# Scale products on GpSimd, two buffers for a split, and one attention step taken apart, in an attention and feed-forward kernel

## The chip, the cores and the metric

The kernel runs on one core of a Trainium2 chip. The metric is device microseconds of one execution: 1246.51 as the median of three runs (1242.34 to 1246.77). One further execution was profiled, and every line of a profile here comes from such an execution.

[...]

## The reference

```python
# q, k, v: (8, 12, 448, 64) float32; w_in (768, 2048), w_out (2048, 768)
scores = scale * np.matmul(q, k.transpose(0, 1, 3, 2)) - np.log(S)   # scale = 1/8, S = 448
attn = 1.0 / (1.0 + np.exp(-scores))
x = np.matmul(attn, v)          # then heads side by side: (3584, 768)
h = x @ w_in
g = h - np.tanh(h)
return g @ w_out
```

Attention with a sigmoid in place of a softmax, in 8 batches of 12 heads, and then a feed-forward layer on the 3584 tokens.

## The kernel before

**Exact products from halves.** A float32 operand is scaled by a power of two and split into two float16 halves, high and low; a product is made as three float16 matmuls (high by high, high by low, low by high) that add up in PSUM. Each operand so needs a scale. For a pair of heads, `norms` (L302) squares q, k and v on ACT with running sums and `scales` (L311) makes the powers of two: PE adds over partitions (`pbn`, L316), ACT applies a Relu (L318), and DVE makes `n_y`, `in`, `sn` and `rn` in five tiny instructions of one to three columns. `parts` (L332) splits K or Q into the tile `w` (one buffer) and has a DMA transpose it; `prep_v` (L348) splits v.

**Stages.** Batch 0's attention is done first, in float32 (`attention32`), while the weights are loaded and converted. Then come, for each batch, the first product (`moe1`, x by w_in, followed by the nonlinearity `mix` on ACT and DVE) and the second (`moe2`, g by w_out). The attention of the next batch is woven into the second product. `stream` (L434) is a generator that yields it in blocks. There are six head pairs in a batch and two blocks to a pair. A block has the scores of two of a pair's four column groups on PE, two sigmoids on ACT (`weigh`) and, from batch 2 on, their splits into `ahl` on ACT and DVE (L382, L383); batch 1's products with v are made in float32. The products of v with finished weights (`do_av`) come in every block for batch 1, and from batch 2 on in a pair's first block (i = 0), for the pair before; after a pair's fourth column group ACT evacuates x and squares it, and POOL adds the squares up (L431). So the last products with v of a batch are in the first block of the next batch's scores.

**The order.** It is written by hand: each of PE, ACT, DVE and POOL runs its instructions in program order. `second` (L937) steps through the second product, one yield for 6 products, and calls the blocks, the tail of `mix` and the preparation of the next x at given steps (`BLOCKS0` in batch 0, `BLOCKS1` in batch 1, `BLOCKS` later). A token tile of 128 tokens ends at steps 16, 32 and 48 in batches 1 to 7: there ACT empties one PSUM tile `po` (L825) and DVE the other (L826); PE has only these two buffers, and goes on into the same two. The last 64 tokens (`por`, L834) fill the rest, at two yields to a step. Three steps after the block that ends a batch's attention, `batch_scales` (L606) makes that batch's scale and splits its six x tiles into `xhl`, the first product's operand. The bound for g, `g_scales` (L631), is worked out after the first `mix`.

**Weights.** w_out is converted during batch 0: `conv_load`, `conv_sign`, `conv_bits`, and a PE product `wl` (L178) for its norm; `w_out_scale` makes its scale and `split` its halves in place, `SHIFT_O` slots ahead of the raw form.

What the diff touches, with the line numbers of the profile:

Of the kernel before, what the change touches and what calls it, by code (L numbers as in the profile page):

```python
# [34 lines left out]
class Builder:  # L35
# [58 lines left out]
    def pow2(self, t, n, tag):  # L94

        nc = self.nc
        y = self.sm.tile([P, n], F32, name=f"{tag}_y", tag=f"{tag}_y")
        nc.vector.tensor_scalar(
            y.bitcast(U32), t.bitcast(U32), 24, 23, op0=ALU.logical_shift_right, op1=ALU.logical_shift_left
        )  # L100
        return y


# [55 lines left out]
    def conv_norm(self, p):  # L159
        nc = self.nc  # L160
        k = p["k"]
        if not p["staged"]:
            return
        p["sq"] = self.sm.tile([P, p["piece"][3]], BF16, name="sq", tag="sq", bufs=4)
# [60 lines left out]
    def scale_of(self, total, tag):  # L225

        nc = self.nc
        t = self.sm.tile([P, 1], F32, name=tag + "_t")
        nc.vector.tensor_scalar(t, total, 2.1, TINY, op0=ALU.mult, op1=ALU.max)
        y = self.pow2(t, 1, tag)  # L230
        inv = self.const.tile([P, 1], F32, name=tag + "_i")
        nc.vector.tensor_scalar(inv, y, 2.0**49, None, op0=ALU.mult)
        S = self.const.tile([P, 1], F32, name=tag + "_s")
        nc.vector.reciprocal(S, inv)
        return S, inv
# [23 lines left out]
    def w_out_scale(self, e):  # L259

        V = self.nc.vector
        m = self.sm.tile([P, 1], F32, name="mo")
        V.tensor_reduce(m, self.wl[:, : self.HALF], axis=AX.X, op=ALU.max)
        total = self.sm.tile([P, 1], F32, name="wtot2")
        V.scalar_tensor_tensor(total, m, 1.05, m, op0=ALU.mult, op1=ALU.mult)
# [36 lines left out]
    def norms(self, loaded):  # L302

        n = len(loaded)
        ss = self.sm.tile([CK, 3], F32, name="ss", bufs=3)
        for i, t in enumerate(loaded):
            junk = self.sm.tile([CK, 8 * D], BF16, name="sqn", tag="sq", bufs=4)
            self.nc.scalar.activation(junk, t.rearrange("p a b d -> p (a b d)"), AF.Square, accum_out=ss[:, i : i + 1])  # L308
        return ss[:, :n]

    def scales(self, ss):  # L311

        nc = self.nc
        n = ss.shape[1]
        pb = self.ps.tile([P, 512], F32, name="pbn", tag="tr", bufs=1)[:, :n]
        nc.tensor.matmul(pb, self.onesf[:CK, :], ss, start=True, stop=True)  # L316
        t = self.sm.tile([P, 3], F32, name="tn")
        nc.scalar.activation(t[:, :n], pb, AF.Relu, bias=self.tiny, scale=2.1)  # L318
        y = self.pow2(t[:, :n], n, "n")
        i = self.sm.tile([P, 3], F32, name="in")  # L320
        nc.vector.tensor_scalar(i[:, :n], y, 2.0**49, None, op0=ALU.mult)
        s = self.sm.tile([P, 3], F32, name="sn", bufs=3)
        nc.vector.reciprocal(s[:, :n], i[:, :n])
        r = self.sm.tile([P, 2], F32, name="rn", bufs=5)
        nc.vector.scalar_tensor_tensor(
            r[:, 0:1], i[:, 0:1], 1.0 / math.sqrt(D), i[:, 1:2], op0=ALU.mult, op1=ALU.mult
        )
        if n == 3:
            nc.vector.tensor_scalar(r[:, 1:2], y[:, 2:3], 2.0**49 / A_SCALE, None, op0=ALU.mult)
        return s, r  # L330

    def parts(self, n, s, name, act):  # L332

        nc = self.nc
        flat = n.rearrange("p c h d -> p (c h d)")
        w = self.qk.tile([CK, 2, 4 * P], F16, name="w", tag="w", bufs=1)
        if act:
            nc.scalar.activation(w[:, 0], flat, AF.Copy, scale=s[:CK])  # L338
# [95 lines left out]
    def stream(self):  # L434
# [171 lines left out]
    def batch_scales(self, xs):  # L606
# [3 lines left out]
        t1 = lambda name: self.sm.tile([P, 1], F32, name=name)  # L610
        tx = t1("tx")
        V.tensor_scalar(tx, m, 2.12, TINY, op0=ALU.mult, op1=ALU.max)
        y = self.pow2(tx, 1, "x")
        ix = t1("ix")
        V.tensor_scalar(ix, y, 2.0**49, None, op0=ALU.mult)
        Sx = t1("Sx")
        V.reciprocal(Sx, ix)
        xhl = []
        for j, x in enumerate(xs):
# [5 lines left out]
            xhl.append(hl)  # L625
        ih, ihk = t1("ih"), t1("ihk")
        V.tensor_tensor(ih, ix, self.iSwi, op=ALU.mult)
        V.tensor_scalar(ihk, ih, KAPPA, None, op0=ALU.mult)
        self.xready = (xhl, ih, ihk, m)

    def g_scales(self, m):  # L631

        t1 = lambda name: self.sm.tile([P, 1], F32, name=name)
        V = self.nc.vector
# [7 lines left out]
        V.scalar_tensor_tensor(h3, h2, 1.0 / 9.0, hc, op0=ALU.mult, op1=ALU.mult)  # L642
        g2 = t1("g2")
        V.tensor_tensor(g2, hb, h3, op=ALU.min)
        V.tensor_scalar(g2, g2, 2.1, TINY, op0=ALU.mult, op1=ALU.max)
        y = self.pow2(g2, 1, "g")
        iSg = t1("iSg")
        V.tensor_scalar(iSg, y, 2.0**49, None, op0=ALU.mult)
        Sg = t1("Sg")
        V.reciprocal(Sg, iSg)  # L650
        return Sg, iSg
# [9 lines left out]
    def moe1(self, st):  # L661

        nc = self.nc
        S = self.S
        xhl, ih, ihk, m = st
        self.gs = []
        self.late = []
        for k in range(self.NF // 2):
# [18 lines left out]
            for _ in self.tail:  # L687
                pass
            if k == 0:
                self.Sg, self.iSg = self.g_scales(m)  # L690

    def moe1_32(self, xs, weights, rest):
# [6 lines left out]
        for k in range(self.NF // 2):  # L699
            ph = self.ps.tile([P, 2, 512], F32, name="ph", tag="sc", bufs=2)  # L700
            for e in range(2):
# [17 lines left out]
                elif (k, e) == (1, 0):  # L719
                    next(w, None)  # L720
                    self.Sg, self.iSg = self.g_scales(m)
                if e == 0 and k in self.INIT:
# [47 lines left out]
    def moe2(self, b, gs):  # L770
# [3 lines left out]
        n = 1 if b == 0 else 3  # L774
        nc.vector.tensor_scalar(iK[:, :n], self.iSwo[:, :n], self.iSg, None, op0=ALU.mult)
        H = self.HALF
# [27 lines left out]
        if b == 0:  # L804
            for e in range(2):
                for tk in range(nt):
                    po = {e: self.ps.tile([P, 512], F32, name="po", tag="mm", bufs=2)}
                    for f in range(0, self.NF, 2):
                        products(po, tk, f, (e,))
                        products(po, tk, f + 1, (e,))  # L810
                        if f + 2 == self.NF:
                            if (e, tk) == (1, 0):
                                nc.vector.tensor_scalar(iK[:, 1:], self.iSwo[:, 1:], self.iSg, None, op0=ALU.mult)
                            o = self.op.tile([P, H], F32, name="oh", tag="o", bufs=2)
# [67 lines left out]
    def first(self, rest):  # L882

        n = 4
        next(self.tail)
        ahead = [self.split_w_out(0)]
        for k in range(n):
# [11 lines left out]
        next(rest)  # L899
        assert n + len(self.BLOCKS0) + len(self.BLOCKS1) == 4 * self.NP + len(self.BLOCKS) - self.ALONE  # L900
        split = self.split_w_in()
# [35 lines left out]
    def second(self, b, blocks, alone, events):  # L937
# [49 lines left out]
```

## Time and profile before

| | us |
|---|---|
| median of three runs | 1246.51 (1242.34 to 1246.77) |
| profiled execution, whole | 1250.16 |
| its span, first to last instruction | 1247.9 |
| PE busy in the span | 1202.3 |
| DVE busy | 941.6 |
| ACT busy | 942.0 |
| POOL busy | 38.0 |

The span is what the rows of the profile cover; 2.26 us of the execution lie around it. Batch 0 with the weights takes until 276 us, where batch 1's first product starts; later batches take some 142 us each. A row of a timeline has the start, the duration (of several alike together, with their count), the engine, the line of the kernel, the operation, output and inputs, and in brackets how long the engine had stood idle and which instruction ended the wait. A row of waits has the waiting engine and line, the instruction that released it, and the sum, the count and the longest in us. A row of a window has the window, its length, the busy time of PE, PE's weight loads, DVE, ACT and POOL, then the granted TensorE clock (1.00 is full speed), the transfers' share and GB/s.

### The profile page before, as it was taken

The page shows a single profiled execution, that of the slowest core. Times are in us where ns is not written, and L with a number is a line of the kernel's source. Part 1 is how long each engine was busy: PE and PEld are TensorE (multiplying, and loading weights), DVE is VectorE, ACT ScalarE, POOL GpSimd, SP SyncE. Part 2 cuts the span into 40 slices and gives each one's busy share as a digit, 9 for nine tenths or more (in the row PEclk, how much of TensorE's full clock was granted, in tenths as well). Part 3 has the DMA queues.
Part 4 walks back from the last instruction along what each step waited for, and adds up shares of the span by engine and source line. Part 5 has one row for each costly group of instructions (what it writes and reads, how often), then busy time and mean ns, then how long its engine had stood idle before and what let it go on. Part 6 is the DMA issues. An engine that isn't in the chain of part 4 may idle for free.

```text
span 1247.9 us, 19830 instructions
## 1 busy us (share of the span) xinstructions
PE 1202.3 (96%) x7675; PEld 651.9 (52%) x7675; DVE 941.6 (75%) x1473; ACT 942.0 (75%) x1325; POOL 38.0 (3%) x38
## 2 busy tenths in 40 slices
PE   9889887999999999999999999999999999999998
PEld 3235433455555555555555555555555655555555
DVE  4879987888966798668976789668985789636930
ACT  5857796967998688886888788886888877864820
POOL 0100000000000000100001000000000000000000
PEclk9999989999999999999999999999999999999999
DMA  9963358220044400432034400552024410300001
GB/s 241 282 171 83 89 124 208 64 61 8 4 111 100 92 1 13 107 93 57 1 65 108 95 2 1 102 110 57 1 55 100 89 25 1 72 21 20 1 14 32
DMA packets 192317, 89.76 MB, mean 72 GB/s; under 512 B 169824, under 2 KB 182368, under 8 KB 192224
## 3 DMA queue, kind: packets, MB, share of 16 engines
q1 hardware_dynamic: 191296, 88.28, 30.4%
q8 instruction: 60, 0.98, 0.3%
q10 hardware_dynamic: 928, 0.23, 0.1%
q14 instruction: 33, 0.27, 0.1%
HBM read 58.20 MB, written 11.01 MB: 55 GB/s over the span
## 4 chain that ended last, share of the span: by engine, by line
PE 71%; DVE 11%; ACT 10%; DMA 4%; issue 3%; SPq 1%; DVEq 0%; ACTq 0%
PE ph L674 31%; PE po L796 22%; PE sc L367 6%; PE acc L391 5%; PE por L834 5%; DMA raw<-moe_w_in 2%; ACT a L376 2%; ACT ahl L382 1%; ACT sqn L308 1%; DVE ahl L383 1%; DVE m L748 1%; DVE m L762 1%; DVE m L759 1%; DVE g L659 1%; DMA K<-w 1%
## 5 line engine op out<-in xcount | busy, mean ns | idle before, releaser
L796 PE MATMUL po<-wo,g 128*128 128x384 f16 x2304 | 394.1, 327 | 7.5 <-DVE o L826 4.9
L674 PE MATMUL ph<-xhl,wi 128*128 128x448 f16 x2016 | 382.6, 352 | 0.0
L796 PEld LDWEIGHTS <-g 128*128 128x128 f16 x2304 | 220.1, 98 | 183.5 <-issue 43.4
L674 PEld LDWEIGHTS <-wi 128*128 128x128 f16 x2016 | 196.7, 98 | 185.0 <-issue 1.8
L383 DVE SCALAR_TENSOR_TENSOR ahl<-a,ahl 112x896 f16<-112x896 f32 x144 | 155.7, 1122 | 68.6 <-ACT ahl L382 68.5
L376 ACT ACTIVATE a<-sc,nls,rn 112x896 f32<-112x896 f32 x168 | 179.5, 1092 | 18.7 <-PE sc L367 18.2
L744 ACT ACTIVATE u<-ph,ih 128x896 f32<-128x896 f32 x64 | 64.4, 1006 | 91.6 <-PE ph L674 87.9
L382 ACT ACTIVATE ahl<-a 112x896 f16<-112x896 f32 x144 | 128.3, 941 | 0.1
L367 PE MATMUL sc<-Q,K 64*112 64x448 f16 x1008 | 116.2, 361 | 8.9 <-ACT a L376 7.3
L748 DVE SCALAR_TENSOR_TENSOR m<-ph,ihk,u 128x896 f32<-128x896 f32 x64 | 73.4, 1147 | 38.0 <-ACT th L746 37.7
L658 ACT ACTIVATE g<-m,Sg 128x896 f16<-128x896 f32 x64 | 66.7, 1042 | 32.7 <-DVE m L762 27.3
L391 PE MATMUL acc<-ahl,vhl 112*64 112x448 f16 x864 | 89.0, 355 | 0.8 <-DVE ahl L383 0.8
L367 PEld LDWEIGHTS <-K 64*112 64x112 f16 x1008 | 60.9, 128 | 47.5 <-issue 27.8
L341 DVE SCALAR_TENSOR_TENSOR w<-qn,sn,w 112x512 f16<-112x512 f32 x42 | 31.5, 750 | 70.5 <-ACT w L338 70.2
L762 DVE COPY_PREDICATED m<-u,th 128x896 f32<-128x896 uint32 x64 | 77.3, 1208 | 6.6
L659 DVE SCALAR_TENSOR_TENSOR g<-m,Sg,g 128x896 f16<-128x896 f32 x64 | 73.3, 1146 | 8.5 <-ACT g L658 8.4
L704 PE MATMUL ph<-x,wi 128*128 128x448 f32 x192 | 76.5, 549 | 0.0
L759 DVE SCALAR_TENSOR_TENSOR m<-q,m 128x896 f32<-128x896 f32 x64 | 70.0, 1093 | 8.3 <-ACT q L758 1.2
L749 DVE SCALAR_TENSOR_TENSOR th<-ph,ih,th 128x896 f32<-128x896 f32 x64 | 73.2, 1143 | 0.0
L761 ACT ACTIVATE u<-u,b 128x896 f32<-128x896 f32 x64 | 66.8, 1044 | 6.4 <-DVE m L748 4.4
L755 DVE SCALAR_TENSOR_TENSOR m<-q,m 128x896 f32<-128x896 f32 x64 | 69.5, 1086 | 0.0
L391 PEld LDWEIGHTS <-vhl 112*64 112x64 f16 x864 | 46.0, 110 | 40.6 <-issue 13.4
(130 smaller groups left out, 1236.3 us busy)
## 6 DMA issues: line engine op xcount, KB each, us to landing
raw<-moe_w_in SPq DMA_DIRECT2D x24, 512.0 KB, 8.3
rawo<-moe_w_out SPq DMA_DIRECT2D x32, 384.0 KB, 4.1
kn<-k SPq DMA_DIRECT2D x96, 112.0 KB, 2.8
vn<-v SPq DMA_DIRECT2D x48, 224.0 KB, 3.1
qn<-q SPq DMA_DIRECT2D x94, 112.0 KB, 2.9
out<-o SPq DMA_DIRECT2D x7, 336.0 KB, 2.7
out<-o SPq DMA_DIRECT2D x7, 288.0 KB, 2.7
out<-o SPq DMA_DIRECT2D x7, 240.0 KB, 3.2
```

The costliest lines, as they stand in the source:

```text
L367: nc.tensor.matmul(ps[:CK, h, :S], K[r, w, cs], Q[r, x, :], start=(n == 0), stop=(n == len(prods) - 1))
L376: nc.scalar.activation(a, ps[:CK, :, :S], AF.Sigmoid, bias=self.nls[:CK], scale=scale)
L382: nc.scalar.activation(A[:, 0], a, AF.Copy, scale=A_SCALE)
L383: nc.vector.scalar_tensor_tensor(A[:, 1], a, A_SCALE, A[:, 0], op0=ALU.mult, op1=ALU.subtract)
L391: nc.tensor.matmul(acc[h * D : (h + 1) * D, : self.S], v[:, w, h, c, :], A[:, x, h], start=(c == 0 and n == 0), stop=(c == 3 and n == 2),)
L659: nc.vector.scalar_tensor_tensor(g[:, 1], m, Sg, g[:, 0], op0=ALU.mult, op1=ALU.subtract)
L674: nc.tensor.matmul(ph[:, e, :S], self.wi[:, c * self.NB + k, part, e * P : (e + 1) * P], xhl[c][:, x, :], start=(i == 0), stop=(i == 3 * s ...
L704: nc.tensor.matmul(ph[:, e, :S], self.where("in", c)[:, f * P : (f + 1) * P], xs[c], start=(c == 0), stop=(c == self.NC - 1),)
L748: V.scalar_tensor_tensor(m, ps, ihk, u, op0=ALU.mult, op1=ALU.mult)
L759: V.scalar_tensor_tensor(m, q2, C2, m, op0=ALU.add, op1=ALU.mult)
L762: V.copy_predicated(m, u.bitcast(U32), th)
L796: nc.tensor.matmul(po[i][:, :H], gs[f // 2][:, x, f % 2, tk * P : (tk + 1) * P], self.wo[:, i * self.NF + f, w], start=(f == 0 and n == 0) ...
```

## The change

- The constants of the scale chains are made from the power of two `y` by one bitwise xor on DVE and products on GpSimd (`over`, and `V = nc.gpsimd` in `scales`, `scale_of`, `w_out_scale`, `batch_scales`, `g_bound`, `g_scales`, `moe2`), in place of a reciprocal and products on DVE.
- `scales` for the pair after next is called in a pair's first block, behind `do_av` and ahead of `prep_v`, in place of at the start of its second block.
- `g_scales` is cut in two, `g_bound` (GpSimd) and `g_scales`, and both are called in `batch_scales` ahead of the splits of x. The splits then follow 1, 3 and 5 steps after the norms in place of 0, 2 and 4.
- `w` shares two buffers of another pool with the squares of the weight conversion; the discarded squares of `norms` go to PSUM; `SHIFT_O` is 4.
- `w_out_scale(0)` is called after the first part of the last `mix` in place of ahead of it.
- Batch 1's last products with v are a step of their own, without scores, and the block with batch 2's first scores comes as the first block of batch 1's second product: `BLOCKS1` has one more entry.

```diff
-    BLOCKS1 = (4, 7, 10, 13, 16, 20, 24, 28, 32, 36, 40, 44, 48, 52)
+    BLOCKS1 = (4, 7, 10, 13, 16, 19, 22, 25, 28, 32, 36, 40, 44, 48, 52)
-    SHIFT_O = 3
+    SHIFT_O = 4
...
+    def over(self, out, y):
+
+        z = self.sm.tile([P, 3], F32, name="z")[:, : y.shape[1]]
+        self.nc.vector.tensor_scalar(z.bitcast(U32), y.bitcast(U32), 0x7F800000, None, op0=ALU.bitwise_xor)
+        self.nc.gpsimd.tensor_scalar(out, z, 2.0**-50, None, op0=ALU.mult)
...
+        junk = self.ps.tile([P, 512], F32, name="sqn", tag="tr", bufs=1)
         for i, t in enumerate(loaded):
-            junk = self.sm.tile([CK, 8 * D], BF16, name="sqn", tag="sq", bufs=4)
...
+        V = nc.gpsimd
         y = self.pow2(t[:, :n], n, "n")
+        s = self.sm.tile([P, 3], F32, name="sn", bufs=3)
+        self.over(s[:, :n], y)
         i = self.sm.tile([P, 3], F32, name="in")
-        nc.vector.tensor_scalar(i[:, :n], y, 2.0**49, None, op0=ALU.mult)
-        s = self.sm.tile([P, 3], F32, name="sn", bufs=3)
-        nc.vector.reciprocal(s[:, :n], i[:, :n])
+        V.tensor_scalar(i[:, :n], y, 2.0**49, None, op0=ALU.mult)
...
-        w = self.qk.tile([CK, 2, 4 * P], F16, name="w", tag="w", bufs=1)
+        w = self.sm.tile([CK, 2, 4 * P], F16, name="w", tag="sq", bufs=2)
...
             for i in range(2):
-                if i:
-                    scales(g + 2)
                 pss = [self.scores(c, K[g], Q[g]) for c in (2 * i, 2 * i + 1)]
...
                 if i == 0 or not splits(g):
                     do_av()
                 if i == 0:
+                    scales(g + 2)
                     if g == 0:
                         prep_v(0)
                     prep_v(g + 1)
...
                 yield 2750, True
+                if i and g == NP - 1:
+                    do_av()
+                    yield 1900, False
...
+        ih, ihk = t1("ih"), t1("ihk")
+        G.tensor_tensor(ih, ix, self.iSwi, op=ALU.mult)
+        G.tensor_scalar(ihk, ih, KAPPA, None, op0=ALU.mult)
+        g = self.g_bound(m)
+        yield 0
+        sg = self.g_scales(g)
         xhl = []
...
-            if k == 0:
-                self.Sg, self.iSg = self.g_scales(m)
...
-                    self.w_out_scale(0)
...
         next(self.tail)
+        self.w_out_scale(0)
...
-            events += [(p, lambda: next(scales[0], None)) for p in (end + 5, end + 7)]
+            events += [(p, lambda: next(scales[0], None)) for p in (end + 4, end + 6, end + 8)]
```

More of the change, by code (lines that the diff above doesn't have):

```diff
@@ L94, in pow2 @@
     def pow2(self, t, n, tag):
-        nc = self.nc
         y = self.sm.tile([P, n], F32, name=f"{tag}_y", tag=f"{tag}_y")
-        nc.vector.tensor_scalar(
+        self.nc.vector.tensor_scalar(
             y.bitcast(U32), t.bitcast(U32), 24, 23, op0=ALU.logical_shift_right, op1=ALU.logical_shift_left
@@ L163, in conv_norm @@
             return
-        p["sq"] = self.sm.tile([P, p["piece"][3]], BF16, name="sq", tag="sq", bufs=4)
+        if k % 2 == 0:
+            self.sq2 = self.sm.tile([P, 2, p["piece"][3]], BF16, name="sq", tag="sq", bufs=2)
+        p["sq"] = self.sq2[:, k % 2]
         if k % 6 == 1:
@@ L611, in batch_scales @@
         tx = t1("tx")
+        G = self.nc.gpsimd
         V.tensor_scalar(tx, m, 2.12, TINY, op0=ALU.mult, op1=ALU.max)
         y = self.pow2(tx, 1, "x")
+        Sx = t1("Sx")
+        self.over(Sx, y)
         ix = t1("ix")
-        V.tensor_scalar(ix, y, 2.0**49, None, op0=ALU.mult)
-        Sx = t1("Sx")
-        V.reciprocal(Sx, ix)
+        G.tensor_scalar(ix, y, 2.0**49, None, op0=ALU.mult)
+        ih, ihk = t1("ih"), t1("ihk")
[4 more added lines that the diff above has]
+        sg = self.g_scales(g)
         xhl = []
@@ L625, in batch_scales, with g_bound @@
             xhl.append(hl)
[L626 to L631, printed above, removed]
+        self.xready = (xhl, ih, ihk, sg)
+    def g_bound(self, m):
         t1 = lambda name: self.sm.tile([P, 1], F32, name=name)
-        V = self.nc.vector
+        V = self.nc.gpsimd
         hb = t1("hb")
@@ L641, in g_scales @@
         h3 = t1("h3")
-        V.scalar_tensor_tensor(h3, h2, 1.0 / 9.0, hc, op0=ALU.mult, op1=ALU.mult)
+        V.tensor_scalar(h3, h2, hc, 1.0 / 9.0, op0=ALU.mult, op1=ALU.mult)
         g2 = t1("g2")
-        V.tensor_tensor(g2, hb, h3, op=ALU.min)
+        V.tensor_scalar(g2, hb, h3, None, op0=ALU.min)
         V.tensor_scalar(g2, g2, 2.1, TINY, op0=ALU.mult, op1=ALU.max)
+        return g2
+    def g_scales(self, g2):
+        t1 = lambda name: self.sm.tile([P, 1], F32, name=name)
+        V = self.nc.gpsimd
         y = self.pow2(g2, 1, "g")
+        Sg = t1("Sg")
+        self.over(Sg, y)
         iSg = t1("iSg")
         V.tensor_scalar(iSg, y, 2.0**49, None, op0=ALU.mult)
-        Sg = t1("Sg")
-        V.reciprocal(Sg, iSg)
         return Sg, iSg
@@ L664, in moe1 @@
         S = self.S
-        xhl, ih, ihk, m = st
+        xhl, ih, ihk, (self.Sg, self.iSg) = st
         self.gs = []
@@ L720, in moe1_32 @@
                     next(w, None)
-                    self.Sg, self.iSg = self.g_scales(m)
+                    g2 = self.g_bound(m)
+                elif (k, e) == (1, 1):
+                    self.Sg, self.iSg = self.g_scales(g2)
                 if e == 0 and k in self.INIT:
@@ L774, in moe2 @@
         n = 1 if b == 0 else 3
-        nc.vector.tensor_scalar(iK[:, :n], self.iSwo[:, :n], self.iSg, None, op0=ALU.mult)
+        nc.gpsimd.tensor_scalar(iK[:, :n], self.iSwo[:, :n], self.iSg, None, op0=ALU.mult)
         H = self.HALF
@@ L899, in first @@
         next(rest)
[L900 removed]
+        assert n + len(self.BLOCKS0) + len(self.BLOCKS1) == 4 * self.NP + len(self.BLOCKS) - self.ALONE + 1
         split = self.split_w_in()
```

24 lines of the change are left out of this document (11 added, 13 removed).

## The prediction

> **What bounds the kernel now.** I read the page first, then TensorE's waits, then the order of time around each wait. TensorE (PE) is the bound: it is busy 96% of the span, so a change pays only where PE stands idle or at a low clock, and costs wherever it makes PE stand.
>
> ```profile
> PE 1202.3 (96%) x7675; PEld 651.9 (52%) x7675; DVE 941.6 (75%) x1473; ACT 942.0 (75%) x1325; POOL 38.0 (3%) x38
> ```
>
> ```profile
> PE wl L178 <- DVE stb L152: 8.4, 8, 2.1
> PE sc L367 <- ACT a L376: 7.3, 5, 2.5
> PE sc L578 <- ACT a L376: 5.0, 6, 1.0
> PE po L796 <- DVE o L826: 4.9, 6, 1.3
> ```
>
> These are PE's largest waits. The third is batch 0's own attention, which the change leaves alone. The first two lie in batch 0's later part, while weights are converted. Rows of PE there, after one of ACT:
>
> ```profile
> 194.15 0.72 ACT L338 ACTIVATE w<-kn,sn 112x512 f16<-112x512 f32 x1 [3.65 <-DVE sn L323]
> ```
>
> ```profile
> 162.65 2.49 PE L367 MATMUL sc<-Q,K 64*112 64x448 f16 x12 [1.45 <-DVE th L749]
> ...
> 195.90 0.77 PE L367 MATMUL sc<-Q,K 64*112 64x448 f16 x6 [1.78 <-ACT a L376]
> ...
> 211.00 0.33 PE L178 MATMUL wl<-stb,onesb 128*128 128x384 bf16 x1 [1.35 <-DVE stb L152]
> ...
> 214.49 0.33 PE L178 MATMUL wl<-stb,onesb 128*128 128x384 bf16 x1 [2.18 <-DMA rawo<-moe_w_out]
> 214.75 2.27 PE L367 MATMUL sc<-Q,K 64*112 64x448 f16 x12
> ...
> 253.81 1.34 PE L367 MATMUL sc<-Q,K 64*112 64x448 f16 x12
> ...
> 260.97 0.35 PE L601 MATMUL nm<-x,onesb 128*128 128x448 bf16 x1 [0.94 <-ACT x L422]
> ```
>
> The 12 score matmuls of a block take 1.34 us at full clock (253.81). At 214.75 they take 2.27: after two waits near each other the clock is granted at half:
>
> ```profile
> 216.00:217.00 1.00, 1.00 (x8) 0.27 (x4) 0.88 (x2) 1.00 (x4) 0.00 (x0) 0.50 0.80 116
> ```
>
> The fourth wait above is the end of a token tile in the second product: PE wants the next pair of PSUM tiles, and ACT and DVE have still to empty them. Batch 1 pays most:
>
> ```profile
> 360.56 0.32 PE L796 MATMUL po<-wo,g 128*128 128x384 f16 x1 [1.25 <-ACT o L825]
> ...
> 362.17 5.37 PE L796 MATMUL po<-wo,g 128*128 128x384 f16 x23 [1.28 <-DVE o L826]
> ```
>
> Batch 2 at the same place, one query for each engine:
>
> ```profile
> 500.26 0.48 DVE L353 TENSOR_SCALAR vhl<-vn,sn 112x512 f16<-112x512 f32 x1
> 500.77 0.75 DVE L354 SCALAR_TENSOR_TENSOR vhl<-vn,sn,vhl 112x512 f16<-112x512 f32 x1
> 502.55 2.34 DVE L383 SCALAR_TENSOR_TENSOR ahl<-a,ahl 112x896 f16<-112x896 f32 x2 [1.02 <-ACT ahl L382]
> 504.81 0.60 DVE L826 TENSOR_SCALAR o<-po,iK 128x384 f32<-128x384 f32 x1
> ```
>
> ```profile
> 501.10 0.58 ACT L422 ACTIVATE x<-x 128x448 f32<-128x448 f32 x1
> 501.58 1.78 ACT L382 ACTIVATE ahl<-a 112x896 f16<-112x896 f32 x2
> ```
>
> ```profile
> 505.47 3.90 PE L796 MATMUL po<-wo,g 128*128 128x384 f16 x23 [0.59 <-DVE o L826]
> ```
>
> Here 23 products take 3.90 us; after batch 1's two waits 23 took 5.37, so a half clock costs 1.47 us more. DVE splits v (L353, L354) while ACT is still evacuating x, then idles 1.02 us until ACT's split of a, and only after its own two splits comes the o that PE waits for.
>
> **The change, part by part.** The sum is made against the profiled execution (1250.16 us, span 1247.9, 2.26 around it); that is 3.65 above the median of 1246.51, and I add the difference to the median.
>
> *Scale chains.* Each removes from DVE the products in, sn, rn and adds one xor:
>
> ```profile
> L323 DVE RECIPROCAL sn<-in 128x3 f32<-128x3 f32 (+1 forms) x42 | 7.3, 174 | 1.4
> L321 DVE TENSOR_SCALAR in<-n_y 128x3 f32<-128x3 f32 (+1 forms) x42 | 7.1, 170 | 1.4
> L98 DVE TENSOR_SCALAR n_y<-tn 128x3 uint32<-128x3 uint32 (+1 forms) x42 | 6.7, 160 | 0.0
> ```
>
> The reciprocal and product (0.174 + 0.170) minus a xor like L98's (0.16) give 0.18 us, times 42: 8 us of DVE, somewhat more with the rn rows. No PE wait in the products of batches 2 to 7 is in front of such a chain, so this is hidden under PE's work; I count 0. The same holds for g_scales, which leaves DVE in the first product, where PE waits for nothing.
>
> *Scales half a pair earlier.* In batch 0's later part it pays: ACT stood 3.65 us for sn at 194.15, and PE's 1.78 at 195.90 follows from it. With sn there a block before, that wait goes; ACT runs ahead, so the raw weight at 211.00 (1.35) should come in time. But DVE, which converts one weight piece a step, limits here too, and now stands for the chain behind ACT's evacuation. I take 1.5 of these 3.1.
>
> *w_out_scale(0) behind the last mix:* its chain no longer delays th, 1.45 at 162.65; ACT binds next, so I take 0.9. *Batch 1's last products with v alone:* the squares no longer queue behind the block's two sigmoids and a w, so 0.94 at 260.97 goes: 0.9. The 1.34 of scores moves to batch 1 and costs the same there: 0. With that block go its Q transpose and the loads of the pair three ahead, on SP's queue: they leave batch 0, where SP also feeds raw weights, and are wanted two blocks later in batch 1: 0. A half clock at 214.75 costs at least 2.27 - 1.34 = 0.93; if the waits before it shrink, it goes: 0.9, and about 0.8 of the 2.18. Together **batch 0: -5**, bounds 0 (DVE limits everything) and -9 (1.45 + 1.78 + 1.35 + 2.18 + 0.94 + 0.93 and the rest of the half clock).
>
> *Batch 1's tile end at step 16.* 1.25 + 1.28 + 1.47 = 4.0 us now. The block ahead of it changes from one with evacuation to one with three squares of norms, so ACT's o is no earlier; PE's own work ahead is a products-with-v shorter. Steps of 3 up to 28 keep ACT behind for twice as long. I take **-2**, bounds -4 and +1.
>
> *The order on DVE in batches 1 to 6, which costs.* In a block with evacuation DVE now has the scale chain in front of its split of v, and that chain waits for an ACT Relu put behind the evacuation and its square. So L353 and L354 (1.2 us), which lay in DVE's idle gap, start after 501.68 + Relu + chain (about 0.6): they end near 503.5, and the splits of a, which started at 502.55, start 1.0 later without any collision; 0.55 at least if ACT is a little earlier. And Pool's sum of squares collides:
>
> ```profile
> 202.66 1.14 POOL L431 TENSOR_TENSOR x<-x,x 128x448 f32<-128x448 f32 x1 [14.88 <-ACT x L422]
> ```
>
> ```profile
> 201.21 0.35 DVE L151 TENSOR_SCALAR stb<-stb 128x384 uint32<-128x384 uint32 x1
> ...
> 203.07 0.95 DVE L151 TENSOR_SCALAR stb<-stb 128x384 uint32<-128x384 uint32 x1 [0.32 <-PE po L796]
> ```
>
> A DVE tensor_scalar of 0.35 us took 0.95 beside Pool's sum. L353 would now stand beside that sum: up to 0.6 more, and tiny Pool products, which queue on Pool behind that sum (none in the trace; bounded by 0 and the 1.14 of a whole sum, taken near 0.1 as they have one to three columns) may add some. **Step 16, batches 2 to 6: +1.1 each, 5.5**, bounds 0.55 and 1.9. At step 32 there is some margin:
>
> ```profile
> 388.71 0.60 DVE L826 TENSOR_SCALAR o<-po,iK 128x384 f32<-128x384 f32 x1
> ```
>
> ```profile
> 389.60 4.08 PE L796 MATMUL po<-wo,g 128*128 128x384 f16 x24
> ```
>
> DVE's o ends at 389.31, PE needs the second tile just after 389.60: margin 0.4. **+0.7 each for five batches, 3.5**, bounds 0.1 and 1.5.
>
> *The end of batches 1 to 5.* The splits of x come in three parts at 48, 50, 52 in place of 47, 49, 51, and the last behind the whole block of 52:
>
> ```profile
> 568.12 0.68 DVE L624 SCALAR_TENSOR_TENSOR xhl<-x,Sx,xhl 128x448 f16<-128x448 f32 x1
> ```
>
> ```profile
> 569.53 10.77 PE L674 MATMUL ph<-xhl,wi 128*128 128x448 f16 x56
> ```
>
> The last split ends at 568.80. PE wants the sixth x after 15 matmuls of 10.77 / 56 = 0.19: 572.4. Ahead of the last two x now lie that block's w (0.75, as L354), v (0.48 + 0.75), a (2.3, the L383 row) and chain (0.3), and the block before has the 1.0 delay; the products moved off DVE give back about 1. So the last split ends near 568.8 + 4.6 + 1.0 - 1.0 = 573.4 and its second half is wanted at 572.6; ten dependent Pool products must also be through before DVE's bound for g, which stands ahead of the first x. **+1.5 each, 7.5**, bounds 0.5 and 2.5.
>
> *Two buffers for w, PSUM for the squares' waste, the shift of 4:* ACT's wait for K's transpose goes, under PE's work: 0; uncovered it would give ACT a microsecond a batch.
>
> Sum: -5 - 2 + 5.5 + 3.5 + 7.5 = +9.5, so 1256.
>
> **Rivals.** (1) *Slower, as above*: 1256, own range 1248 to 1267. (2) *Faster*: the stall of ACT for sn and the clock cuts that follow carry the day. Gains at their bounds, -9 and -4, against order costs at their floor, 5 x 0.55 + 5 x 0.1 + 5 x 0.5 = 6: -7, 1239.5. [...] It decides if DVE's o and last x move by less than half a microsecond. Against it: program order puts the split of v behind Relu. (3) *Even*: gains -7, costs at about 7: 1246.5. (4) *Much slower*: the step-16 wait of 0.59 + 1.1 = 1.7 cools the clock as in batch 1, 1.47 more in each of five batches: 1256 + 7 = 1263. Two waits of 1.25 and 1.28 within 2.9 us did it there; one of 1.78 at 195.90 did not.
>
> [...]
>
> **How the numbers follow.** Chances: 0.5 for 1256, 0.17 faster, 0.2 even, 0.13 much slower. What a measurement can tell from no change is 0.5%, 6.2 us: 1240.3 to 1252.7. A seventh of the first case lies under 1252.7 (0.07), rival 3 between, a little of rival 2 above 1240.3: faster 0.16, same 0.28, slower 0.56. The range for 8 in 10 reaches from 1239, inside the faster case, to 1266, past the middle of rival 4.
>
> **What would show it.** Right: PE's wait for DVE's o at step 16 grows from 0.59 to 1.5 or more, one appears at step 32, PE's first L674 of batches 2 to 6 waits for xhl, and L353 stands behind the chain's xor. Also: no ACT wait for sn near 190, no 0.94 at the norms of batch 1. Wrong: those o waits unchanged, the first product starting without a wait, or the half clock gone from batches 0 and 1 altogether.

## The result, and the profile after

The changed kernel takes 1265.86 us (median of four, 1265.32 to 1267.09), the kernel before 1244.97 beside it (1242.34 to 1246.77): a ratio of 1.0178, with a 95% interval of 1.0159 to 1.0197. The forecast had the direction, but +9.5 us where +20.9 came.

In the rows PE is TensorE, DVE VectorE, ACT ScalarE, POOL GpSimd and SP SyncE. The page's busy times and TensorE's waits in the changed kernel (waiting line, releaser, sum, count, longest in us). L813 is the second product (L796 before), L843 DVE's eviction `o` (L826), L373 the scores, L611 the reduction `m` of the norms, L639 the second half of a split of x:

```profile
PE 1210.2 (96%) x7675; PEld 646.2 (51%) x7675; DVE 934.2 (74%) x1260; ACT 946.4 (75%) x1325; POOL 198.5 (16%) x311
```

```profile
PE po L813 <- DVE o L843: 15.8, 10, 2.5
PE wl L185 <- DVE stb L157: 13.6, 10, 4.0
PE sc L373 <- ACT a L382: 4.2, 3, 2.9
PE ph L692 <- DVE xhl L639: 3.4, 10, 0.4
PE sc L373 <- DVE m L611: 2.0, 5, 0.4
```

DVE is less busy (934.2 against 941.6 us) and PE waits longer for it: 15.8 us in ten evictions against 4.9 in six. Two waits are new, for x and for `m`. POOL went from 38.0 to 198.5 us.

Batch by batch, from the start of one first product to that of the next (us, read from PE's timelines). "Before" is a second profile of the unchanged kernel (the run e11 below), because batch 0 took 276.0 in the first one:

| | batch 0 | 1 | 2 | 3 | 4 | 5 | 6 | 7 | span |
|---|---|---|---|---|---|---|---|---|---|
| before | 271.1 | 151.8 | 141.8 | 141.8 | 142.5 | 141.8 | 135.8 | 115.9 | 1242.6 |
| after | 267.0 | 155.9 | 146.8 | 146.8 | 146.8 | 146.8 | 138.5 | 115.9 | 1264.5 |
| difference | -4.1 | +4.1 | +5.0 | +5.0 | +4.3 | +5.0 | +2.7 | 0.0 | +21.9 |

What holds PE at step 16 of batch 2, in four timelines of the changed kernel; the same place as the prediction's rows from 500 to 505 us. DVE:

```profile
495.94 0.75 DVE L347 SCALAR_TENSOR_TENSOR w<-qn,sn,w 112x512 f16<-112x512 f32 x1 [2.46 <-ACT w L344]
498.21 1.06 DVE L97 TENSOR_SCALAR n_y<-tn 128x3 uint32<-128x3 uint32 x1 [1.52 <-ACT tn L325]
499.31 0.17 DVE L105 TENSOR_SCALAR z<-n_y 128x3 uint32<-128x3 uint32 x1
499.38 0.48 DVE L359 TENSOR_SCALAR vhl<-vn,sn 112x512 f16<-112x512 f32 x1
499.90 0.75 DVE L360 SCALAR_TENSOR_TENSOR vhl<-vn,sn,vhl 112x512 f16<-112x512 f32 x1
500.57 2.08 DVE L389 SCALAR_TENSOR_TENSOR ahl<-a,ahl 112x896 f16<-112x896 f32 x2
502.57 0.61 DVE L843 TENSOR_SCALAR o<-po,iK 128x384 f32<-128x384 f32 x1
```

ACT:

```profile
497.45 0.58 ACT L428 ACTIVATE x<-x 128x448 f32<-128x448 f32 x1
497.93 0.25 ACT L325 ACTIVATE tn<-pbn,tiny 128x3 f32<-128x3 f32 x1
```

POOL:

```profile
498.11 1.14 POOL L437 TENSOR_TENSOR x<-x,x 128x448 f32<-128x448 f32 x1 [72.10 <-ACT x L428]
```

PE:

```profile
500.89 0.34 PE L813 MATMUL po<-wo,g 128*128 128x384 f16 x1
...
503.24 3.90 PE L813 MATMUL po<-wo,g 128*128 128x384 f16 x23 [2.00 <-DVE o L843]
```

DVE stands 1.52 us for ACT's Relu, which is behind the evacuation of x and its square. That square also releases POOL's sum, so the sum starts (498.11) with the Relu's end, and the shift `n_y` of three columns, 0.16 us elsewhere, takes 1.06 beside it. The splits of v, in a gap of DVE before, come only at 499.38. The splits of a and `o` follow, and PE waits 2.00 us where it waited 0.59.

Batch 1 lost its two waits at step 16, and has one at step 32; and at batch 3's first product the last x is late (PE in the changed kernel):

```profile
382.08 5.58 PE L813 MATMUL po<-wo,g 128*128 128x384 f16 x23 [2.50 <-DVE o L843]
...
410.23 0.78 PE L373 MATMUL sc<-Q,K 64*112 64x448 f16 x6 [0.41 <-DVE m L611]
...
569.77 2.63 PE L692 MATMUL ph<-xhl,wi 128*128 128x448 f16 x13
572.70 0.84 PE L692 MATMUL ph<-xhl,wi 128*128 128x448 f16 x3 [0.30 <-DVE xhl L639]
```

Here 23 products took 5.58 us instead of 3.90: the granted clock was 0.50 from 383 to 386 us, which costs 1.68. A steady batch's +5.0 is then 1.41 at step 16 (2.00 - 0.59), 0.83 at step 32, 0.67 for x (0.30 and 0.37 in the waits of that batch), 0.41 for `m`, 0.17 for each of four more stops (0.34 + 3.90 against 4.07 us in one piece), and, as an estimate, some 0.6 for `pbn`, which now stands between other products (84 matmuls at 262 ns in place of 216, 3.9 us in seven batches): 4.6 of 5.0.

### The profile page after: what moved, and what is told of

Its sections match the earlier page's. It is cut to its first block, busy times and chain, and to the rows that moved or that the text cites. A ratio compares the mean times of both kernels' runs of the same rounds, so it can differ in the third digit from the quotient of the medians.

```text
span 1264.5 us, 19948 instructions
## 1 busy us (share of the span) xinstructions
PE 1210.2 (96%) x7675; PEld 646.2 (51%) x7675; DVE 934.2 (74%) x1260; ACT 946.4 (75%) x1325; POOL 198.5 (16%) x311
## 4 chain that ended last, share of the span: by engine, by line
PE 59%; DVE 16%; ACT 16%; issue 5%; POOL 2%; DMA 1%; DVEq 0%; ACTq 0%; SPq 0%
PE ph L692 29%; PE po L813 19%; ACT a L382 6%; PE acc L397 4%; PE sc L373 3%; DVE ahl L389 3%; PE por L851 2%; ACT sqn L315 2%; DVE xhl L639 1%; DVE n_y L97 1%; ACT ahl L388 1%; ACT wo L222 1%; DVE xhl L638 1%; ACT w L344 1%; ACT x L428 1%
## 5 line engine op out<-in xcount | busy, mean ns | idle before, releaser
L813 PE MATMUL po<-wo,g 128*128 128x384 f16 x2304 | 395.6, 328 | 17.0 <-DVE o L843 15.8
L813 PEld LDWEIGHTS <-g 128*128 128x128 f16 x2304 | 223.0, 99 | 185.7 <-issue 46.9
L389 DVE SCALAR_TENSOR_TENSOR ahl<-a,ahl 112x896 f16<-112x896 f32 x144 | 150.8, 1088 | 27.1 <-ACT ahl L388 27.1
L373 PE MATMUL sc<-Q,K 64*112 64x448 f16 x1008 | 116.6, 362 | 6.2 <-ACT a L382 4.2
L437 POOL TENSOR_TENSOR x<-x,x 128x448 f32<-128x448 f32 x24 | 27.7, 1155 | 558.4 <-ACT x L428 558.4
L373 PEld LDWEIGHTS <-K 64*112 64x112 f16 x1008 | 60.7, 128 | 58.7 <-issue 37.9
```

Of the source, the lines that this page charges most:

```text
L373: nc.tensor.matmul(ps[:CK, h, :S], K[r, w, cs], Q[r, x, :], start=(n == 0), stop=(n == len(prods) - 1))
L389: nc.vector.scalar_tensor_tensor(A[:, 1], a, A_SCALE, A[:, 0], op0=ALU.mult, op1=ALU.subtract)
L813: nc.tensor.matmul(po[i][:, :H], gs[f // 2][:, x, f % 2, tk * P : (tk + 1) * P], self.wo[:, i * self.NF + f, w], start=(f == 0 and n == 0) ...
```

## The experiments

In all of them the kernel before ran beside the others on the same chip; its medians were 1244.05, 1244.27, 1244.05 and 1247.25 us in the four groups.

### First group: which engine, which place

Two theories at first: the order (scales too early in a block, x splits too late), or the slow products on GpSimd.

**e1, products on VectorE.**

```diff
-        V = nc.gpsimd
+        V = nc.vector
```

(the same in every function that has this line, in `over` and for `iK`)

> The changed kernel with every small product that it put on GpSimd back on VectorE (same order, same split of the scale chain, same buffers and blocks). Two theories for the 20.9 us lost. Order: the scales stand too early in a block and the x splits too late in a batch, whatever engine multiplies; then the three parts of a batch's loss that are read from the waits (step 16 +1.4, step 32 +0.8, first product and its norms +1.6) stay, only some 0.7 us of each of six batches comes back, 1262 us, and PE's waits for the output evictions on VectorE stay near 15.8 us (10 times). GpSimd: the 1.0 to 1.4 us that a product takes there are the loss; then 1238 to 1246 us and that wait falls to the 4.9 us of before.

Measured: 1290.96 us, ratio 1.0377 [1.0349, 1.0405]. Both theories missed: the same order is 25 us worse with the products on VectorE. TensorE's waits in this kernel:

```profile
PE po L813 <- DVE o L843: 22.3, 10, 2.8
...
PE sc L373 <- DVE m L611: 5.3, 5, 1.1
PE ph L692 <- DVE xhl L638: 4.2, 5, 0.8
```

Four products now stand ahead of the splits of v too, and PE's waits for `o`, `m` and `xhl` are all longer (`xhl` 7.9 us with a second row of 3.7, against 3.4). The clock is cut five times in batches 1 to 6 (0.50 granted from 385 to 388 us, for one), against once in the changed kernel. So GpSimd is not the loss; it shelters part of it.

**e2, scales late.** The call goes back to the start of a pair's second block; the products stay on GpSimd.

```diff
             for i in range(2):
+                if i:
+                    scales(g + 2)
...
                 if i == 0:
-                    scales(g + 2)
```

> The changed kernel with the scales of the pair after next back at the start of the block's second half (the products stay on GpSimd). Order: step 16 and step 32 give back 1.4 and 0.8 us and some 0.5 us of displaced pbn products in each of six batches, so about 1250 us; PE's waits for the evictions on VectorE fall from 15.8 to about 5 us. GpSimd: 1262 to 1266 us, as the slow products only move to another place.

Measured: 1257.80 us, ratio 1.0108 [1.0085, 1.0132]. The wait for `o` fell to 4.7 us as the order theory has it, but the time by 8.1 instead of 16, because a wait grew elsewhere. PE, first product of batch 3 in this kernel:

```profile
565.45 2.44 PE L693 MATMUL ph<-xhl,wi 128*128 128x448 f16 x12
568.94 0.35 PE L693 MATMUL ph<-xhl,wi 128*128 128x448 f16 x1 [1.04 <-DVE xhl L639]
569.66 0.84 PE L693 MATMUL ph<-xhl,wi 128*128 128x448 f16 x3 [0.37 <-DVE xhl L640]
570.87 4.47 PE L693 MATMUL ph<-xhl,wi 128*128 128x448 f16 x14 [0.37 <-DVE xhl L640]
```

1.78 us for x here, and 14 products in 4.47 us (0.32 each, against 0.20 in the first row): by this pace, as an estimate, the clock was cut there, and again in batch 5's.

**e3, both edits.**

> Both edits together: scales at the start of the second half and all small products on VectorE. What is left of the change in the later batches is the place of the x splits (one step later, behind the chain for g). Order: that place alone costs the first product's 1.1 us and the norms' 0.5 us in six batches against the gain of batch 0, so 1245 to 1248 us. GpSimd: 1236 to 1240 us, as nothing is left that costs.

Measured: 1260.31 us, ratio 1.0128 [1.0100, 1.0156]: 2.5 us above e2, which is less than its own spread (1257.79 to 1263.32). Neither theory fits: the place of the x splits costs much more than the forecast's 7.5 us once the scales are late.

**e4, x splits back as well.**

```diff
-            events += [(p, ...) for p in (end + 4, end + 6, end + 8)]
+            events += [(p, ...) for p in (end + 5, end + 7)]
...
+            if k == 0:
+                self.Sg, self.iSg = self.g_scales(self.g_bound(m))
```

> As the one before, and the x splits too at their old steps (end+3, +5, +7) with the chain for g back in the first product. Left of the change: the step of batch 1's last products with v, its block list, two buffers for sq and w, the norms' squares into PSUM, the first w_out scale one place later. Both theories: batch 0's gain alone, 9 us in the profiles, so 1236 to 1239 us, if those 9 us are the change's; if the 4.4 us that were gained before 70 us are a difference from run to run, 1240 to 1242 us.

Measured: 1242.46 us, ratio 0.9987 [0.9975, 0.9999]. Steady batches take 142.2 us, near the 141.8 of before. The x splits' part of the change is 17.9 us here, and the gain of batch 0 is small: of its 9 us in the first comparison, 5 belonged to that one profile (e11).

### Second group: the two costs apart

**e5, only the splits back.** The changed kernel with the splits at end+3, +5 and +7; the end of the chain for g then stands in the first product.

> The changed kernel (early scales, products on GpSimd) with the x splits at the steps of before (end+3, +5, +7); the chain for g stays on GpSimd and its last part moves behind the splits, into the first product. Theory that the step of the splits is the largest part: with products on VectorE it was 17.9 us (1260.3 less 1242.5), and the same here gives 1248 us; PE's first product shows no wait for xhl, and the waits for the eviction at steps 16 and 32 (2.8 us a batch) stay. Rival, the waits add up: only the 0.7 us for xhl, the 0.4 us for m and the pipeline's restarts of six batches come back, 1257 us.

Measured: 1265.53 us, ratio 1.0171 [1.0150, 1.0191]. Nothing came back. The waits for x are gone and those for `o` are unchanged; the batches alternate between 145.7 and 147.4 us (146.8 each with the late splits). PE at the tile ends in this kernel:

```profile
502.29 3.90 PE L813 MATMUL po<-wo,g 128*128 128x384 f16 x23 [2.00 <-DVE o L843]
...
648.02 5.58 PE L813 MATMUL po<-wo,g 128*128 128x384 f16 x23 [2.02 <-DVE o L843]
...
795.41 3.90 PE L813 MATMUL po<-wo,g 128*128 128x384 f16 x23 [2.00 <-DVE o L843]
...
941.12 5.58 PE L813 MATMUL po<-wo,g 128*128 128x384 f16 x23 [2.01 <-DVE o L843]
...
1088.53 5.58 PE L813 MATMUL po<-wo,g 128*128 128x384 f16 x23 [2.01 <-DVE o L843]
```

The same wait cuts the clock in three of the five batches, 1.68 us each, and in none of the five of the changed kernel. So 1.1 us a batch was gained (146.8 to 145.7) and three clock cuts, 5.0 us together, took it back.

Why equal waits differ is in the clock's record. In this profile the half clock lasts 3.41 us each time in these batches, and the three cuts begin at 648.26, 941.81 and 1088.58 us, which are 86 and 43 times 3.413 apart. So in this profile the clock changed on a grid of 3.413 us. Two cells of it with the wait and the cell behind each, as rows of a window (here the second number is TensorE's busy time in us, and the clock is the third from the end):

```profile
644.85:648.26 3.41, 1.39 (x13) 0.64 (x10) 3.41 (x5) 3.31 (x5) 2.49 (x3) 1.00 0.41 103
648.26:651.68 3.42, 3.42 (x13) 1.56 (x12) 2.85 (x4) 2.77 (x7) 0.00 (x0) 0.50 1.28 160
...
791.62:795.03 3.41, 1.78 (x15) 0.81 (x14) 3.37 (x6) 3.30 (x5) 2.99 (x4) 1.00 0.51 135
795.03:798.45 3.42, 3.04 (x19) 1.85 (x19) 3.38 (x5) 3.36 (x8) 0.00 (x0) 1.00 0.55 147
```

Where the wait of 2.02 us lies whole in one cell, TensorE is busy for 1.39 us of it and the next cell has half the clock (1.41 in the other two cuts). Where the wait reaches over into another cell, the busy time is 1.78 and the clock stays, as it does in batch 2 (2.19) and at 650.05 in the changed kernel (2.27). In the changed kernel the half clocks of 3.41 us at 215.40 and 382.65 us begin 49 times 3.413 apart, so its clock fits the same grid. A batch there takes 146.8 us, close to 43 cells (146.77), so its waits at step 16 meet the grid at nearly one place from batch to batch, and all five were spared.

**e6, place alone**, and **e7, chain alone**: e4 with one half of the x edit each.

```diff
 e6
+        yield 0
...
-            events += [(p, ...) for p in (end + 5, end + 7)]
+            events += [(p, ...) for p in (end + 4, end + 6, end + 8)]
 e7
+        sg = self.g_scales(self.g_bound(m))
         xhl = []
```

> The kernel of 1242.5 us (scales late, products on VectorE, chain for g in the first product) with one edit: the six x splits at end+4, +6 and +8 instead of end+3, +5 and +7. Place theory: the last pair stands behind the block at step 52 and PE waits for it three times in each first product of batches 2 to 6 (1.3, 0.4 and 0.4 us): 1255 to 1259 us, most of the 17.9 us. Rival, the chain for g ahead of the splits on VectorE does it: 1242 to 1246 us.

> The kernel of 1242.5 us with the other half of that edit: the chain for g (10 small products, some 1.7 us on VectorE) ahead of the x splits, which stay at end+3, +5 and +7. Place theory: 1243 to 1247 us, the chain costs at most its own 1.7 us at the eviction of the second tile (0 to 0.7 us a batch as far as that waited). Rival: 1255 us and more.

Measured: e6 1246.03 us, ratio 1.0012 [0.9999, 1.0025]; e7 1251.53 us, ratio 1.0056 [1.0035, 1.0076]. The place theory of e6 missed by 9 us, and its rival's range ends where the time came out; e7 lies between its two ranges. The steps alone cost 3.6 us above e4, the chain alone 9.1, both together 17.9 (e3 against e4), more than the sum of 12.7; e3 and e4 ran in the first group. In e7 PE waits at another place, for the last `ahl` of the batch, which stands behind the chain on DVE:

```profile
PE acc L397 <- DVE ahl L389: 7.9, 12, 1.2
```

**e8, products on GpSimd with both old places.**

> All small products on GpSimd, scales at the start of the second half, x splits at end+3, +5 and +7, the chain for g on GpSimd from the norms' step and its end in the first product. If a product on GpSimd costs nothing where it is awaited late, as the step from 1260.3 (VectorE) to 1257.8 us (GpSimd) says, this is 1238 to 1241 us, the fastest so far. Rival: the 1.0 to 1.4 us products make sn, rn and iK late once their places are the old ones: 1244 to 1250 us.

Measured: 1239.95 us, ratio 0.9980 [0.9963, 0.9997]. Against e5, which differs only in the call of `scales`, this prices the early scales at 25.6 us, with e5's four clock cuts in batches 1 to 6 among them (some 6.7 us; e8 has none there). With the late x splits the same call is worth 8.1 us only (the changed kernel against e2). Against e4, in another group, the products on GpSimd gain 2.5 us by the medians, but the ratios of 0.9980 and 0.9987 have intervals that overlap, so this gain isn't shown. What a product took on GpSimd differed with the order too. Groups of POOL in the changed kernel, and in e8:

```profile
L333 POOL TENSOR_SCALAR rn<-in 128x1 f32<-128x1 f32 x42 | 58.6, 1395 | 4.1
L335 POOL TENSOR_SCALAR rn<-n_y 128x1 f32<-128x1 f32 x36 | 36.4, 1011 | 2.7
...
L106 POOL TENSOR_SCALAR sn<-z 128x3 f32<-128x3 f32 (+1 forms) x42 | 15.3, 363 | 203.4 <-DVE z L105 203.4
```

```profile
L335 POOL TENSOR_SCALAR rn<-n_y 128x1 f32<-128x1 f32 x36 | 23.8, 660 | 2.7
L333 POOL TENSOR_SCALAR rn<-in 128x1 f32<-128x1 f32 x42 | 14.9, 354 | 4.1
L106 POOL TENSOR_SCALAR sn<-z 128x3 f32<-128x3 f32 (+1 forms) x42 | 9.7, 230 | 440.6 <-DVE z L105 440.6
```

The instruction L333 takes 1395 ns on average in the changed kernel, where DVE's second split of a (L389, two tensors in) runs beside 34 of the 42, and 354 in e8, where DVE's first split of K (L346, one tensor in) runs beside 38.

### Third group: why the early scales cost

**e9, scales behind the splits of v** (on e5).

```diff
                 if i == 0:
-                    scales(g + 2)
...
                     prep_v(g + 1)
+                    scales(g + 2)
```

> The kernel of 1265.5 us (early scales, products on GpSimd, x splits at the old steps) with one edit: the call of scales for the pair after next stands behind prep_v in the same block, no longer ahead of it. Theory: the early scales cost 25.6 us (1265.5 less 1239.95) because on VectorE the two splits of v (1.2 us) queue behind the chain's first part, which waits for ScalarE's Relu (1.5 to 1.9 us) and then stands 0.9 us longer beside GpSimd's sum; with v ahead of it the splits of v go back into VectorE's idle gap, the wait at step 16 falls from 2.0 to about 0.8 us, that at step 32 goes, and so do the clock cuts of 1.7 us: 1243 to 1250 us. Rival: the places on TensorE and ScalarE (the norms' product ahead of the second product's work, Relu between evacuation and the splits of a) cost it: 1258 us or more.

Measured: 1244.16 us, ratio 1.0000 [0.9987, 1.0013]: two calls in another order, and 21.4 us less than e5, which ran in the second group. DVE, batch 3, and then PE's row at step 16:

```profile
634.18 0.48 DVE L359 TENSOR_SCALAR vhl<-vn,sn 112x512 f16<-112x512 f32 x1
634.69 0.75 DVE L360 SCALAR_TENSOR_TENSOR vhl<-vn,sn,vhl 112x512 f16<-112x512 f32 x1
635.78 1.06 DVE L97 TENSOR_SCALAR n_y<-tn 128x3 uint32<-128x3 uint32 x1 [0.34 <-ACT tn L325]
```

```profile
639.62 3.90 PE L813 MATMUL po<-wo,g 128*128 128x384 f16 x23 [0.80 <-DVE o L843]
```

The shift still takes 1.06 us, but v is through: the wait for `o` is 0.80 us, and no clock cut is left in batches 1 to 6 (1.00 granted throughout). The rival is excluded as the main cause; TensorE and ScalarE have the same early places here.

**e12, no sum** (on e5): GpSimd's sums of squares for the second to fourth pair are left out, so x's norm misses pairs.

> The kernel of 1265.5 us with GpSimd's sums of squares left out for the second to fourth pair of each batch (the norm of x is then of two or three pairs only; this part of the computation is missing). The 128x3 shift ahead of the splits of v, which took 1.06 us beside that sum, takes 0.16 us if it is the sum that blocks it; then the waits at steps 16 and 32 shrink by 0.9 and 0.8 us in batches 2 to 6 and the time falls to some 1252 to 1257 us. If the shift stays at 1 us, something else holds it, and the time stays at 1265 us.

Measured: 1247.06 us in one execution, 18.5 below e5's median and below the 1252 to 1257 expected. The tile `n_y` in e5, then in e12 (duration minimum/median/maximum in ns):

```profile
L97 DVE TENSOR_SCALAR n_y<-tn x42: 145/1056/1130, 109.7 to 1099.2; 128x3 uint32<-128x3 uint32 x36, 128x2 uint32<-128x2 uint32 x6
```

```profile
L97 DVE TENSOR_SCALAR n_y<-tn x42: 153/169/1118, 108.7 to 1080.2; 128x3 uint32<-128x3 uint32 x36, 128x2 uint32<-128x2 uint32 x6
```

It is POOL's sum that holds the shift, the waits at step 16 fall from 2.0 to 1.1, those at step 32 go in batches 2 to 6, and the clock cuts with them. PE at step 16 of batch 2:

```profile
495.42 3.90 PE L816 MATMUL po<-wo,g 128*128 128x384 f16 x23 [1.11 <-DVE o L846]
```

Some 4 us of the 18.5 lie in batch 0, as the sums are missing there too. The rows of the changed kernel say the same: 24 of its 42 shifts run beside a sum of 1.13 to 1.15 us, take 1.05 to 1.13 us and end 0.02 to 0.04 us after it, and the other 18 take 0.16 to 0.19. Why the shift lasts as long as the sum, no row shows.

**e10, the step of products with v alone** (on the kernel before), with its block list.

> The kernel before with one part of the change: batch 1's last products with v as a step of their own, the block with batch 2's first scores in batch 1's second product, and the block list that goes with it. Where the prediction had -0.9 us in batch 0 and -2 us in batch 1: 1241 to 1242 us if that holds; 1244 us if, as the kernels with late scales say (batch 1 took 151.7 us in them and before), batch 1 gains nothing.

Measured: 1243.07 us, ratio 0.9988 [0.9972, 1.0003], within noise. In its profile batch 0 is 1.3 us shorter than in e11, as much as the 1.34 us of scores that moved away; batch 1 takes 151.6 us against 151.8. Its waits at step 16 have gone to step 32, where they are 0.42 and 1.22 us and cut nothing.

**e11, the kernel before again.**

> The kernel before, unchanged, profiled once more, to see how far its batch 0 differs from run to run. The first profile's execution was 1250.2 us, against a median of 1244.3 us. If batch 0 (276.0 us there, 267 to 270.5 us in the kernels with the change) comes out at 270 to 272 us, the change's true gain in batch 0 is 2 to 4 us and half of the 9 us was a slow run; at 275 us or more it is the change's.

Measured: 1244.84 us, batch 0 at 271.1 us: 5 us of the 276.0 in the first profile were that run's, and the change gains 4.1 in batch 0, by one profile of each kernel.

### Fourth group: the order alone, and a better kernel

**e13, the early scales alone on the kernel before.** The edit of e2 the other way round, nothing on GpSimd.

> The kernel before with one edit: scales for the pair after next behind do_av and ahead of prep_v in a pair's first block. Nothing goes to GpSimd, the x splits keep their steps. Theory: this order alone is the loss, whatever else the change has; with products on VectorE it was 30.7 us between the kernels of 1260.3 and 1291.0 us, on GpSimd 25.6 us, so 1265 to 1275 us, with the waits for the eviction near 2.8 us at step 16 and 1.4 at step 32. Rival: it needs the rest of the change (buffers, block list, later x splits) to cost that much: 1250 to 1258 us, near the 9 us that the forecast had for steps 16 and 32.

Measured: 1278.36 us, ratio 1.0252 [1.0224, 1.0279], 31 us slower, and above the 1265 to 1275 expected. The profiled execution was the shortest of the four (1273.30). TensorE's waits in it have the signature of the change:

```profile
PE po L795 <- DVE o L825: 20.6, 11, 2.9
...
PE sc L367 <- DVE m L602: 4.6, 5, 1.5
```

The shift `n_y` takes 1.05 us here as the median, against 0.16 in the kernel before. So it lasts that long beside GpSimd's sum (1.11 us at 650.22, a sum of 1.14 at 650.16), which the kernel before has too, without any product on GpSimd.

**e14, early scales for batch 1's pairs alone** (on e8): early and behind `prep_v` while batch 0's products run, where no v is split; late afterwards.

> The kernel of 1239.95 us (products on GpSimd, late scales, old steps of the x splits) with the scales early, and behind prep_v, for the six pairs of batch 1 alone, whose blocks lie in batch 0's time where no v is split. In the profiles batch 0 took 266.2 and 267.4 us with early scales and 268.5 to 270.5 with late ones: if the 2 us are the early scales', 1237 to 1239 us; if they are chance or belong to something else, 1239 to 1241 us.

Measured: 1238.38 us (1237.25 to 1239.63), ratio 0.9938 [0.9920, 0.9957] to the kernel before in its group: the fastest of all. Batch 0 took 265.0 us in its profile, 268.5 in e8's; against e8's median the difference is 1.6 us across two groups, so the size of this last gain is not settled.

## Why the prediction was right or wrong

**Where the sum failed.** The direction and the mechanism on DVE were right, and the signs that were named for it came: the wait for `o` at step 16 grew to 2.00 us, one of 0.83 appeared at step 32, the first products wait for `xhl`, and the split of v stands behind the xor. The size was wrong, in two places. Batches 0 and 1 had -7 in the sum and gave 0.0 (-4.1 and +4.1 against e11), and batches 2 to 6 had +16.5 and gave +22.0. These two misses, 12.5 us, are the difference between the +9.5 of the forecast and the +21.9 of the profiles, within rounding. That the time still lies in the range up to 1266 us is luck: batch 1 went past its own bound of +1, and the clock cuts that stand for the upper end did not come in batches 2 to 6.

**Batch 1: -2 forecast, +4.1 measured.** This step had the wrong sign. The heading said batches 1 to 6, but the sum counted the cost of the order in five batches, 2 to 6, and for batch 1 a gain alone. The two waits at step 16 and their clock cut did go, 4.2 us. The same order cost a wait of 2.50 us and a clock cut of 1.68 at step 32, since the blocks woven into batch 1 already split v; with the late scales of e8 the waits there are 0.61 and 1.23 us, without a cut. The margin of 0.4 that was taken for step 32 was read from rows of batch 1, and charged to the other five. The scores moved from batch 0 added 1.34. Waits for `m` and for the splits of a, 0.4 more each, are part of the rest.

**The order on DVE, steps 16 and 32: mechanism right, price too small.** It named the shift behind Relu, the splits of v behind the shift, the sum's collision and the late `o`. The waits were +1.1 and +0.7 in the sum and +1.41 and +0.83 in the profile. The blocked instruction was another one: not the split of v was stretched but the 3-column shift ahead of it, by 0.9 us instead of up to 0.6. What failed is the count of what follows from these waits. A steady batch had 3.3 us in the sum and cost 5.0, though the wait for x was 0.67 in place of 1.5: missing were 0.41 for `m`, which comes later from the same DVE, 0.68 for the stops' own restarts and some 0.6 for `pbn` between products. Alone, the early scales have no single price. The forecast had 9.0 us for them; the changed kernel against e2 gives 8.1, and e5 against e8 25.6 by the medians and 24.6 in the profiles, batch by batch 4.1, 3.8, 5.4, 3.8, 5.5 and 3.1 (less 1.1 in batch 0).

**The end of a batch: +7.5 forecast.** The mechanism, the last x behind the block at step 52, is in the rows (xhl after 569.77). Its price depends on the rest: 17.9 us with late scales (e3 against e4, and e2 against e8), nothing measurable with early ones (the change against e5). Part of this is shown, the wait for x being 1.78 us in e2 and 0.67 in the changed kernel and the clock cuts falling differently; a single number for this edit doesn't exist. Together the early scales and the end of the batch had 16.5 us in the sum and cost 25.9 (the changed kernel against e8), batch 1 included. The chain for g ahead of the splits, to which the forecast gave a clause and no price, is the dearer half where the scales are late and the products on VectorE (e7).

**Products on GpSimd "taken near 0.1 us".** By line and kernel they took 0.23 to 1.4 us on average, past the bound of 1.14. It did not matter for the sign: in the order of the change GpSimd is ahead of VectorE by 25.1 us (e1), and in the two other pairs of runs by 2.5 us each, which their spread doesn't let be called shown.

**Batch 0: -5 forecast, -4.1 measured**, which is in part luck. 1.34 us of it are the scores that only moved to batch 1, and which the forecast counted as 0. The wait for `sn` near 190 is gone, as is the one for `th`. The 0.94 at the norms stayed in the changed kernel (1.20 there), a half clock at 216 us (0.50 granted) stayed, and the wait for the weights grew (13.6 us, against 7.6 in e11 and 2.2 more there for their transfer). The attention of batch 0, "which the change leaves alone", waited 1.4 us for its sigmoids instead of 4.0; in e13, which has the early scales alone, it waited 1.4 too, and in e10 1.9, so no edit can be named for that.

**Rival 4, the clock.** It was given 0.13 and 1.47 us a batch. In the changed kernel waits of 2.00 and 2.01 us cut nothing in batches 2 to 6, but the same waits did so three times in five in e5. So that none came here was a matter of where the waits fell, not of their length. The cuts after 2.01 and 2.02 us came behind cells of 3.413 us in which TensorE was still busy for 1.39 and 1.41 us. A wait of 1.7 us that lies whole in a cell was in none of these rows, so what it does stays open.

## What to carry to other kernels

On an engine that works in program order, as VectorE did here (the shift ahead of the splits of v at 498.21 us, behind them at 635.78 with the two calls exchanged), look at what an instruction waits for before moving it ahead of others: a 0.16 us shift that waited for a late Relu, and then stood beside GpSimd's sum, pushed everything behind it, and moving two calls past each other was worth 21 us (e9 against e5). Price an edit that makes waits by all that follows from them (restarts, clock, the next waits on the same engine), and in every stage that has the order, the first one too. Where two edits load the same engine, measure them together and apart, since their costs do not add.

## What the runs showed of the hardware

In e5 equal waits of TensorE, 2.00 to 2.02 us, cut the clock in three batches and not in two others, at 1.68 us each time. The granted clock changed there on a grid of 3.413 us, and it fell to 0.50 behind a cell in which TensorE was busy for 1.39 or 1.41 us, not behind one with 1.78 or 2.19. In the changed kernel a VectorE shift over three columns took 1.06 us beside a GpSimd sum of 1.14 us, and 0.17 without (498.21 and 552.90 us). And the other way round a GpSimd product of one column took 354 ns where a VectorE split with one tensor as input mostly ran beside it, and 1395 ns where one with two did, as means of 42.
